# Weights issued later, block sums taken earlier, and half of one batch's q turned by DMA instead of TensorE

## The chip, the cores and the metric

One core of a Trainium2 chip. The metric is device time in microseconds (us) of one execution. Every run is listed with its granted TensorE clock (1.0 is full speed). Runs are sorted into fast and slow (slow: over 1.5% above the fastest run of the same kernel).

## The reference, cut to what matters

```python
# q, k, v: (4 batches, 8 heads, 768 positions, 64), float32
k_sum = k.reshape(B, H, 24, 32, D).max(axis=3)      # one key per block of 32
v_sum = v.reshape(B, H, 24, 32, D).mean(axis=3)     # one value per block
scores = [scale * q @ k.T  where |i - j| < 16,  scale * q @ k_sum.T + log(32)]
a = softmax(scores);  x = a @ [v, v_sum]            # (3072 tokens, 512)
h = x @ w_in                                        # w_in: 512 x 2048
out = (h * sigmoid(1.702 * h)) @ w_out              # w_out: 2048 x 512
```

Attention is sparse and small; the two dense products are what TensorE spends its time on (of the chain that ended last in the kernel before, `h` has 33.4% and `out` 36.4%).

## The kernel before

The tokens are taken in eight half-batches of 384, called stages 0 to 7. Each stage is a first layer (`ph`, 64 matmuls) and an output product (`po`, 48). Attention of the next half-batch is threaded between the steps of the output product. Each engine has its own instruction order, and in the traces it keeps to it (SP before, stages 1 and 2: k from 68.22 us, v from 75.17, k's transposes from 84.32, x's from 92.29, as the program has them). SP (SyncE) issues nearly all transfers, also the DMA transposes that turn q, k and x.

The opening, in GpSimd's order: two weight chunks go out between value casts.

```python
    load_w_in(0)                 # GpSimd issues the transfer
    s_mask(1, dve)
    v_even(1, "dve_alone")
    s_exp(2)
    load_w_in(1)
    v_before(2, pool)            # a cast on GpSimd that waits for value rows
# ... last value casts on GpSimd, each behind its transfer ...
    load_w_in(2); load_w_in(3); load_q(0, p, 1); load_w_out(0..3)
```

Batch 1's q is turned on TensorE in stage 1 (24 turns of 128 x 128, six per head pair: three for each half of the positions); batches 2 and 3 use SP transposes:

```python
    def tq1(p, eng):                       # batch 1, head pair p
        big = psb.tile([128, 1024], F32, name="ps_q", tag="big")
        for half in range(2):
            for r in range(JH):            # JH = 3
                pe.matmul(out=big[...], lhsT=src[:, r]..., rhs=ident)
        copy(eng, qT[p][1]..., big...)
    # plan1: which attention piece stands behind which step of stage 1's output product
    plan1 = {0: ["t0"], 1: ["t1"], 2: ["s0", "s1"], 4: ["t2"], 5: ["t3"], ..., 9: ["v1", "S0", "S1"], 11: ["x1"]}
```

And SP's order in an odd stage: k of the next batch behind step 1, its v behind step 7, then k's transposes, then the transposes of this attention's x (`xT`), which the next first layer reads.

The softmax here doesn't subtract the row's maximum and nothing guards it: scores larger than these inputs give would overflow.

Of the kernel before, what the change touches and what calls it, by code (L numbers as in the profile page):

```python
# [34 lines left out]
def kernel(  # L35
# [16 lines left out]
    NP = H // 2  # L52
# [45 lines left out]
    def load_q(b, p, half=None):  # L98
        if half is None:
            t = stage.tile([128, 2, NJ, D], F32, name=f"qf{p}", tag=f"qf{p}0")  # L100
            sp.dma_start(out=t.rearrange("p h j d -> p (h j) d"), in_=chunks(q, b, p))
            raw["q", p] = t
            return
        if half and p == 0:
            late[0] = stage.tile([128, NP, 2, JH, D], F32, name="qfl", tag="qfl")
            if b == 0:
                pool.dma_start(out=late[0].rearrange("p i h r d -> p (i h) (r d)"),
                               in_=q[0, :, HALF:S].rearrange("h (p r) d -> p h (r d)", r=JH))
        t = (late[0][:, p] if half else
             stage.tile([128, 2, JH, D], F32, name=f"qf{p}0", tag=f"qf{p}0"))  # L110
        raw["q", p, half] = t
        if b == 0 and half:
            return
        sp.dma_start(out=t.rearrange("p h r d -> p h (r d)"),
                     in_=q[b, 2 * p:2 * p + 2, half * HALF:(half + 1) * HALF]
                     .rearrange("h (p r) d -> p h (r d)", r=JH))
# [135 lines left out]
    def copy(eng, out, in_):  # L252
        if eng is act:
            act.activation(out=out, in_=in_, func=ACT.Copy)
        elif eng == "dve_alone":

            dve.tensor_reduce(out=out, in_=in_.unsqueeze(len(in_.shape)), axis=AX.X, op=ALU.max)
        else:
            eng.tensor_copy(out=out, in_=in_)
# [13 lines left out]
        cast["k", p] = t  # L273

    def cast_q1(p):
        for half in range(2):
            cast_q(pool, p, half)
            cast["q", p, half] = cast.pop(("q", p))

    def cast_q(eng, p, half=None):  # L280
        if half is None:
            if p % 2 == 0:
                qb2[p // 2] = castp2.tile([128, 2, NJ, 2, D], BF16, name="qb", tag="qb")
            t = qb2[p // 2][:, p % 2]
        else:
            t = castp.tile([128, JH, 2, D], BF16, name="qb", tag="qb")
        copy(eng, t.rearrange("p r h d -> p h r d"),
             raw[("q", p) if half is None else ("q", p, half)])
        cast["q", p] = t
# [207 lines left out]
    def b_exp(g):  # L497
        ab = st["ab", g] = attp.tile([128, HALF], BF16, name="ab", tag="ab")
        act.activation(out=ab, in_=st["B", g][:, 0:HALF], func=ACT.Exp, scale=scale)

    def v_own(p, hh, eng):

        copy(eng, rows_of(0, p, hh)[:, :, 1], raw_v(p, hh))
# [4 lines left out]
    def v_before(p, eng):  # L508

        copy(eng, rows_of(0, p)[96:128, 1:JH, 0], raw_v(p)[96:128, 0:JH - 1])  # L510
# [97 lines left out]
        key_rows(p, s, ks)  # L608

    def tq1(p, eng):  # L610
        big = psb.tile([128, 1024], F32, name="ps_q", tag="big")
        for half in range(2):
            src = cast.pop(("q", p, half))
            for r in range(JH):
                o = half * 512 + r * 128
                pe.matmul(out=big[:, o:o + 128], lhsT=src[:, r].rearrange("p h d -> p (h d)"),
                          rhs=ident, start=True, stop=True)
        copy(eng, qT[p][1].rearrange("p (e c r) -> p e r c", e=2, r=JH),
             big.rearrange("p (e x) -> p e x", e=2)[:, :, 0:HALF]
             .rearrange("p e (r c) -> p e r c", r=JH))  # L620

    a_sb, x_sb, x2 = {}, {}, {}

# [189 lines left out]
    v_own(1, 1, "dve_alone")  # L813
    av_near(0)
    av_blocks(0, 0, D + 1)
    load_w_in(0)
    s_mask(1, dve)
    v_even(1, "dve_alone")
    s_exp(2)
    load_w_in(1)  # L820
    v_before(2, pool)
    v_sum(1)
    v_copy(1, act)
    v_own(2, 1, "dve_alone")
# [55 lines left out]
    for p in range(NP):  # L880
# [2 lines left out]



    plan = {0: ["s0", "s1"], 3: ["v0", "s2", "s3"], 4: ["d0"], 5: ["v1", "S0", "S1", "d1"]}
    odd = {0: ["v0", "s2", "s3"], 1: ["d0"], 3: ["v1", "d1"]}

    plan1 = {0: ["t0"], 1: ["t1"], 2: ["s0", "s1"], 4: ["t2"], 5: ["t3"],
             6: ["v0", "s2", "s3"], 8: ["x0"], 9: ["v1", "S0", "S1"], 11: ["x1"]}  # L890

    plan0 = {-1: ["q0", "q1", "q2", "q3", "s0", "s1"], 3: ["v0", "s2"], 5: ["x0", "s3"], 7: ["v1"], 9: ["x1"]}

# [1 line left out]

    def beside(u, slot):
        b, half = u // 2, u % 2
        for what in (plan0 if u == 1 else plan1 if u == 2 else odd if half else plan).get(slot, ()):
            i = int(what[1])
            if what[0] == "t":  # L900
                tq1(i, dve if i % 2 else act)
            elif what[0] == "q":
                q_turn(i, 1)
                q_copy(i, dve, 1)
            elif what[0] == "s":
                scores(b, half, i)
                if half and i == NP - 1:
                    gelu_soon()
            elif what[0] == "S":
                scores(b, 1, i)  # L910
                if i == 1:
                    gelu_soon()
            elif what[0] == "v":
                values(b, half, i, u == 1)
            elif what[0] == "d":
                dx(i)
            else:
                tx(i)
# [25 lines left out]
    for u in range(2 * B):  # L944
        b, half = u // 2, u % 2
        todo = {}
        if u == 0:
            for p in range(NP):
                todo.setdefault(12 + p // 2, []).append(lambda p=p: cast_q(dve, p, 1))
        elif u == 1:  # L950
            s = 1
            todo = {2: [lambda: tk(0, s)], 4: [lambda: tk(1, s)],
                    6: [lambda: tk(2, s)], 8: [lambda: tk(3, s)],
                    14: [lambda: halo_odd(w51, 0), lambda: vsum(s, range(NJ))],
                    15: [lambda: block_sums(), lambda: halo_even(w51, 0),
                         lambda: sum_dmas(w51, 0)]}
            for p in range(NP):
                cast_k(pool, p)
            for p in range(NP):
                cast_v(pool, s, p, 0)  # L960
                cast_v(pool, s, p, 1)
            for p in range(NP):
                cast_q1(p)
        elif half == 0 and b + 1 < B:
            todo = {0: [lambda: turn_keys(u, b + 1)]}
        elif b + 1 < B:
            s = (b + 1) % 2
            todo = {0: [lambda: turn_queries(u, s)],
                    1: [lambda: rest_k(0, s)], 3: [lambda: rest_k(1, s)],
                    6: [lambda: rest_k(2, s)], 8: [lambda: rest_k(3, s)]}  # L970
        if u == 1:
            for p in range(NP):
                clear_kx(pool, p, 0)
            clear_vw(pool, 0)
        if u:
            ff_in(u, range(3))
        for nt in range(0 if u else N0, NT):
            if u == 0 or nt > 2:
                ff_in(u, (nt,))
            for f in todo.get(nt, ()):  # L980
                f()
        nxt = u + 1 < 2 * B
        if nxt:
            exp_soon()
        if u == 0:
            beside(1, -1)
            busy(6)
        i = 0
        order = [(ms, part) for ms in range(JH) for part in range(4)]
        if u == 0:  # L990

            order = [(ms, part) for part in range(4) for ms in range(JH)]
        for ms, part in order:
            if nxt or ms < JH - 1:
                ff_out(u, ms, part)
            elif part == 0:
                ff_last(u, ms)
            if nxt:
                beside(u + 1, i)
            i += 1  # L1000
            if u == 0 and i == 1:

                sp.dma_start(out=hold, in_=w_out_sb[0:16, NT - 5, 0:16])
                for p in range(NP):
                    load_k(1, p)
                load_v(1)
                for p in range(NP):
                    load_q(1, p, 0)
                    load_q(1, p, 1)
            elif half and b + 2 < B and i == 1:  # L1010
                for p in range(NP):
                    load_k(b + 2, p)
            elif half and b + 2 < B and i == 7:
                load_v(b + 2)
            elif half == 0 and 0 < b < B - 1 and i == 7:
                for p in range(2, NP):
                    load_q(b + 1, p)
            elif half == 0 and 0 < b < B - 1 and i == 10:
                s = (b + 1) % 2
                vsum(s, range(NJ))  # L1020
                block_sums()
                w5 = vw[s].rearrange("p (j e) h c -> p j e h c", e=2)
                halo_dmas(w5, 0)
                sum_dmas(w5, 0)
# [30 lines left out]
```

## Time and profile before

| | kernel before |
|---|---|
| median, range | 219.09 us, 217.85 to 220.0 (3 runs) |
| profiled span | 218.5 us, clock 0.998 |
| TensorE busy | 205.6 us, 94% |
| idle of TensorE one can name | 1.9 (value rows), 0.5 (w_in), 0.6 (q's copy) us |

The prediction below shows the lines. Lines of SP's queue give start, time held, queue, kind, tiles, count.

### The profile page before, as it was taken

How to read it: one execution, taken by the hardware profiler on the slowest of the kernel's cores; microseconds unless marked ns; L12 is line 12 of the kernel's file. 1: busy time of each engine (PE TensorE's matmuls, PEld its weight loads, DVE VectorE, ACT ScalarE, POOL GpSimd, SP SyncE). 2: the span in 40 equal slices, each digit the busy share in tenths (PEclk: the TensorE clock that was granted, in tenths of full speed). 3: DMA queues.
4: the chain of work that ended last, by engine and by line, in shares of the span. 5: the costliest groups of instructions: out<-in, count | busy, mean ns of one | idle time of the engine just before them, and what ended most of it. 6: DMA issues, size and time to landing. Idle time of an engine off the chain costs nothing.

```text
span 218.5 us, 4915 instructions
## 1 busy us (share of the span) xinstructions
PE 205.6 (94%) x1927; PEld 116.0 (53%) x1950; DVE 91.0 (42%) x262; ACT 135.5 (62%) x242; POOL 68.8 (32%) x169
## 2 busy tenths in 40 slices
PE   7785998999999999999999999999999999999994
PEld 3354655456655555545555465545655555456542
DVE  5897708443964840336707300619228003300000
ACT  2797868156578397842786677815787578437420
POOL 5684988014974019500600069004100000000000
PEclk9999999999999999999999999999999999999999
DMA  5999999999998999899799999989904300520012
GB/s 163 317 217 195 139 263 215 192 196 218 233 352 196 225 252 236 142 221 226 148 204 222 217 227 194 205 194 204 197 3 104 115 0 3 120 92 7 0 48 96
DMA packets 92710, 37.15 MB, mean 170 GB/s; under 512 B 77856, under 2 KB 89568, under 8 KB 92688
## 3 DMA queue, kind: packets, MB, share of 16 engines
q1 hardware_dynamic: 88272, 31.87, 71.0%
q0 software_dynamic: 4416, 4.98, 13.2%
q8 instruction: 15, 0.25, 0.5%
q14 instruction: 7, 0.06, 0.1%
HBM read 27.26 MB, written 6.29 MB: 154 GB/s over the span
## 4 chain that ended last, share of the span: by engine, by line
PE 79%; DMA 10%; SPq 6%; issue 2%; POOL 2%; DVE 1%; POOLq 0%; DVEq 0%
PE po L27 36%; PE ph L27 33%; DMA w_out_sb<-in_moe_w_out_dram 7%; SPq L27 6%; PE ps_av L27 3%; DMA vf<-in_v_dram 3%; PE ps_s L27 3%; PE ps_t L27 1%; DVE qT L27 1%; POOL w_in_sb L27 1%; PE ps_q L27 1%; PE ps_vs L27 1%; PE ps_x L27 1%; POOL vw L27 0%; POOL qfl L27 0%
## 5 line engine op out<-in xcount | busy, mean ns | idle before, releaser
L27 PE MATMUL po<-w_out_sb,gT 128*128 128x512 bf16 (+2 forms) x377 | 85.7, 370 | 2.4 <-issue 1.8
L27 PE MATMUL ph<-xT,w_in_sb 128*128 128x384 bf16 x512 | 85.8, 326 | 0.5 <-DMA w_in_sb<-in_moe_w_in_dram 0.5
L27 ACT ACTIVATE gT<-ph 128x384 bf16<-128x384 f32 x128 | 61.1, 491 | 23.1 <-PE ph L27 23.1
L27 PEld LDWEIGHTS <-w_in_sb 128*128 128x128 bf16 x512 | 49.6, 98 | 33.8 <-DMA w_in_sb<-in_moe_w_in_dram 1.1
L27 PEld LDWEIGHTS <-gT 128*128 128x128 bf16 x400 | 36.5, 98 | 39.1 <-issue 0.3
L27 ACT ACTIVATE osb<-po 128x512 f32<-128x512 f32 (+1 forms) x24 | 14.1, 589 | 35.0 <-PE po L27 33.6
L27 ACT ACTIVATE a_sb<-ps_s 128x768 bf16<-128x768 f32 x32 | 24.3, 804 | 12.7 <-PE ps_s L27 12.4
L27 DVE RECIPROCAL rc<-ps_av 128x6 f32<-128x6 f32 x32 | 6.1, 190 | 50.5 <-PE ps_av L27 50.4
L27 POOL CAST vw<-vf 128x768 bf16<-128x768 f32 (+4 forms) x35 | 24.7, 765 | 5.0 <-DMA vf<-in_v_dram 3.8
L27 DVE TENSOR_TENSOR a_sb<-a_sb,mk 128x768 bf16<-128x768 bf16 x32 | 17.9, 563 | 17.5 <-ACT a_sb L27 15.9
L27 ACT ACT_TABLE_LOAD x16 | 20.5, 1283 | 1.1 <-PEq L1039 0.8
L27 POOL COPY gate<-gT 128x1 bf16<-128x1 bf16 x4 | 0.8, 192 | 60.2 <-ACT gT L27 60.2
L27 DVE TENSOR_TENSOR x<-ps_av,rc 128x384 bf16<-128x384 f32 x28 | 15.6, 558 | 1.0
L27 POOL CAST kb<-kf 128x768 bf16<-128x768 f32 (+1 forms) x15 | 11.1, 768 | 15.5 <-DMA kf<-in_k_dram 15.5
L27 PEld LDWEIGHTS <-a_sb 128*64 128x64 bf16 x384 | 8.0, 111 | 6.4 <-issue 3.1
L27 DVE COPY osb<-po 128x128 f32<-128x128 f32 x1 | 0.3, 292 | 26.6 <-PE po L27 26.6
L27 DVE TENSOR_REDUCE ks<-kx 128x24 bf16<-128x768 bf16 x12 | 11.2, 938 | 0.1
L27 PE MATMUL ps_s<-qT,kx 64*128 64x64 bf16 x384 | 9.3, 191 | 1.0 <-DVE qT L27 0.6
L27 PE MATMUL ps_av<-vw,a_sb 128*64 128x65 bf16 x384 | 10.0, 197 | 0.1
L27 POOL CAST qb<-qf 128x768 bf16<-128x768 f32 (+1 forms) x14 | 9.4, 698 | 1.5 <-DMA qf<-in_q_dram 0.9
L27 DVE COPY kx<-kx 128x80 bf16<-128x80 bf16 (+4 forms) x50 | 9.6, 287 | 0.0
L27 PEld LDWEIGHTS <-kx 64*128 64x128 bf16 x384 | 7.0, 95 | 3.8 <-issue 3.0
(71 smaller groups left out, 121.6 us busy)
## 6 DMA issues: line engine op xcount, KB each, us to landing
out_dram<-osb SPq DMA_DIRECT2D x23, 256.0 KB, 3.3
kf<-in_k_dram SPq DMA_DIRECT2D x12, 384.0 KB, 5.5
vf<-in_v_dram SPq DMA_DIRECT2D x12, 384.0 KB, 6.3
qf<-in_q_dram SPq DMA_DIRECT2D x8, 384.0 KB, 4.9
w_in_sb<-in_moe_w_in_dram POOLq DMA_DIRECT2D x4, 512.0 KB, 8.2
w_out_sb<-in_moe_w_out_dram POOLq DMA_DIRECT2D x4, 512.0 KB, 16.2
kf<-in_k_dram SPq DMA_DIRECT2D x8, 192.0 KB, 3.9
qf<-in_q_dram SPq DMA_DIRECT2D x8, 192.0 KB, 5.3
```

The lines of the kernel that those rows point to most:

```text
L27: r = f(*a, **kw)
```

## The change

Its intent: keep the weights out of the way of the last value rows (the "hold-back" below), take twelve transposes and half of each of four PSUM copies out of TensorE's full stage (the late half of batch 1's q, "late q" below, goes by DMA), and move one block of scores and the block sums to places where nobody waits for them. Its core (the copies of the plans and the cast are cut):

```diff
+    def pool_waits(p):
+        pool.tensor_copy(out=gate2, in_=a_sb[p][:, 0, 0, 0:1])   # a gate: one column
...
+    s_mask(1, dve)
+    pool_waits(1)
     load_w_in(0)
-    s_mask(1, dve)
     v_even(1, "dve_alone")
     s_exp(2)
+    v_before(2, pool)
     load_w_in(1)
-    v_before(2, pool)
...
+    def xq1(p):                                   # late half of batch 1's q, pair p
+        sp.dma_start(out=qT[p][1][:, HALF:S]..., in_=late_q(p)..., transpose=True)
...
     def tq1(p, eng):                              # now 3 matmuls, not 6
...
-    plan1 = {0: ["t0"], 1: ["t1"], 2: ["s0", "s1"], 4: ["t2"], 5: ["t3"],
-             6: ["v0", "s2", "s3"], 8: ["x0"], 9: ["v1", "S0", "S1"], 11: ["x1"]}
+    plan1 = {0: ["t0", "t1"], 2: ["s0", "s1"], 4: ["t2", "t3"],
+             6: ["v0", "s2", "s3"], 8: ["x0"], 9: ["v1"], 11: ["x1"]}
+    plan3 = {2: ["s0", "s1"], 4: ["v0", "s2", "s3"], 5: ["d0"], 6: ["v1", "d1"]}
...
-            busy(6)                               # six filler matmuls in the opening
...
             elif half and b + 2 < B and i == 1:
+                if u == 1:                        # stage 1
+                    for p in range(NP):
+                        load_q(1, p, 1)           # three transfers on SP
                 for p in range(NP):
                     load_k(b + 2, p)
+                if u == 1:
+                    for p in range(NP):
+                        cast_q1(p)
+                        xq1(p)                    # four transposes on SP, three tiles each
...
+            elif half == 0 and 0 < b < B - 1 and i == (6 if u == 2 else 4):
+                vsum((b + 1) % 2, range(NJ))      # was at step 10, with the sums
```

More of the change, by code (lines that the diff above doesn't have):

```diff
@@ L112, in load_q @@
         if b == 0 and half:
+            return
+        if half:
+            if p == 0:
+                for r in range(JH):
+                    o = HALF + r * 128
+                    sp.dma_start(out=late[0][:, :, :, r].rearrange("p i h d -> p (i h) d"),
+                                 in_=q[b, :, o:o + 128].rearrange("h p d -> p h d"))
             return
@@ L275, in cast_q1, with late_q @@
     def cast_q1(p):
-        for half in range(2):
-            cast_q(pool, p, half)
-            cast["q", p, half] = cast.pop(("q", p))
+        if p == 0:
+            qb2[0] = castp2.tile([128, 2, NJ, 2, D], BF16, name="qb", tag="qb")
+        pool.tensor_copy(out=late_q(p).rearrange("p r h d -> p h r d"), in_=raw["q", p, 1])
+    def late_q(p):
+        return qb2[0][:, p // 2, p % 2 * JH:p % 2 * JH + JH]
+    def xq1(p):
+        sp.dma_start(out=qT[p][1][:, HALF:S].rearrange("p (j c) -> p j c", c=128),
+                     in_=late_q(p).rearrange("p r h d -> p (r h d)"), transpose=True)
     def cast_q(eng, p, half=None):
@@ L610, in tq1 @@
     def tq1(p, eng):
-        big = psb.tile([128, 1024], F32, name="ps_q", tag="big")
-        for half in range(2):
-            src = cast.pop(("q", p, half))
-            for r in range(JH):
-                o = half * 512 + r * 128
-                pe.matmul(out=big[:, o:o + 128], lhsT=src[:, r].rearrange("p h d -> p (h d)"),
-                          rhs=ident, start=True, stop=True)
-        copy(eng, qT[p][1].rearrange("p (e c r) -> p e r c", e=2, r=JH),
-             big.rearrange("p (e x) -> p e x", e=2)[:, :, 0:HALF]
-             .rearrange("p e (r c) -> p e r c", r=JH))
+        ps = pmm.tile([128, 512], F32, name="ps_q", tag="mm")
+        src = cast.pop(("q", p))
+        for r in range(JH):
+            pe.matmul(out=ps[:, r * 128:r * 128 + 128],
+                      lhsT=src[:, r].rearrange("p h d -> p (h d)"), rhs=ident, start=True, stop=True)
+        copy(eng, qT[p][1][:, 0:HALF].rearrange("p (c r) -> p r c", r=JH),
+             ps[:, 0:HALF].rearrange("p (r c) -> p r c", r=JH))
     a_sb, x_sb, x2 = {}, {}, {}
@@ L882 @@
     clear_vw(pool, 1)
-    plan = {0: ["s0", "s1"], 3: ["v0", "s2", "s3"], 4: ["d0"], 5: ["v1", "S0", "S1", "d1"]}
+    plan = {1: ["s0", "s1"], 3: ["v0", "s2", "s3"], 4: ["d0"], 5: ["v1", "S0", "S1", "d1"]}
+    plan3 = {2: ["s0", "s1"], 4: ["v0", "s2", "s3"], 5: ["d0"], 6: ["v1", "d1"]}
     odd = {0: ["v0", "s2", "s3"], 1: ["d0"], 3: ["v1", "d1"]}
-    plan1 = {0: ["t0"], 1: ["t1"], 2: ["s0", "s1"], 4: ["t2"], 5: ["t3"],
-             6: ["v0", "s2", "s3"], 8: ["x0"], 9: ["v1", "S0", "S1"], 11: ["x1"]}
+    plan1 = {0: ["t0", "t1"], 2: ["s0", "s1"], 4: ["t2", "t3"],
+             6: ["v0", "s2", "s3"], 8: ["x0"], 9: ["v1"], 11: ["x1"]}
     plan0 = {-1: ["q0", "q1", "q2", "q3", "s0", "s1"], 3: ["v0", "s2"], 5: ["x0", "s3"], 7: ["v1"], 9: ["x1"]}
@@ L897, in beside @@
         b, half = u // 2, u % 2
-        for what in (plan0 if u == 1 else plan1 if u == 2 else odd if half else plan).get(slot, ()):
+        for what in (plan0 if u == 1 else plan1 if u == 2 else plan3 if u == 3 else odd if half else plan).get(slot, ()):
             i = int(what[1])
@@ L906, in beside @@
                 scores(b, half, i)
-                if half and i == NP - 1:
+                if i == NP - 1 and (half or b == 1):
                     gelu_soon()
@@ L962 @@
             for p in range(NP):
-                cast_q1(p)
+                cast_q(pool, p, 0)
         elif half == 0 and b + 1 < B:
@@ L1008 @@
                     load_q(1, p, 0)
-                    load_q(1, p, 1)
             elif half and b + 2 < B and i == 1:
+                if u == 1:
+                    for p in range(NP):
+                        load_q(1, p, 1)
                 for p in range(NP):
                     load_k(b + 2, p)
+                if u == 1:
+                    for p in range(NP):
+                        cast_q1(p)
+                        xq1(p)
             elif half and b + 2 < B and i == 7:
@@ L1017 @@
                     load_q(b + 1, p)
+            elif half == 0 and 0 < b < B - 1 and i == (6 if u == 2 else 4):
+                vsum((b + 1) % 2, range(NJ))
+            elif half == 0 and 0 < b < B - 1 and i == (8 if u == 2 else 5):
+                block_sums()
             elif half == 0 and 0 < b < B - 1 and i == 10:
                 s = (b + 1) % 2
-                vsum(s, range(NJ))
-                block_sums()
                 w5 = vw[s].rearrange("p (j e) h c -> p j e h c", e=2)
```

## The prediction

> **What bounds the kernel now.** I read the busy shares first, then the chain that ended last in order of time, then every idle stretch of TensorE, then the DMA issues with their landings.
>
> ```profile
> span 218.5 us, 4915 instructions
> PE 205.6 (94%) x1927; PEld 116.0 (53%) x1950; DVE 91.0 (42%) x262; ACT 135.5 (62%) x242; POOL 68.8 (32%) x169
> PE 79%; DMA 10%; SPq 6%; issue 2%; POOL 2%; DVE 1%; POOLq 0%; DVEq 0%
> ```
>
> TensorE (PE) is busy 94% of the span and is 79% of the chain; only about 13 us of idle are left. The chain says where a gain can be had. Its early part:
>
> ```profile
> 14.12 6.10 DMA vf<-in_v_dram
> ...
> 20.27 0.52 POOL vw L27
> ...
> 20.84 0.34 PE ps_vt L27 x3
> ...
> 21.30 0.50 POOL vw L27
> 21.80 1.44 POOL w_in_sb L27 x2
> 23.23 0.90 POOL qfl L27
> ...
> 24.85 15.31 DMA w_out_sb<-in_moe_w_out_dram
> 40.16 0.04 issue
> 40.20 1.02 PE po L27 x4
> ```
>
> The last value rows (vf) land at 20.22, GpSimd (POOL) casts them, and only behind that cast does it issue the last two chunks of w_in, the late q and all of w_out. Chunk 2 of w_out lands at 40.16 and TensorE goes on there. The 15.31 us is not one transfer's length: the chunk stands in a queue behind four others. From 40.2 on the chain is TensorE nearly all the way, except here:
>
> ```profile
> 64.44 0.86 PE po L27 x4
> 65.30 0.35 PE ps_q L27 x6
> 65.65 0.02 issue
> 65.67 1.46 DVE qT L27
> 67.13 0.04 issue
> 67.17 0.35 PE ps_s L27 x12
> ```
>
> This is the output product of the second half-batch (stage 1; stages count half-batches from 0), with batch 1's attention interleaved. Scores wait for VectorE to copy the transposed q out of PSUM. TensorE's own list of idle times agrees:
>
> ```profile
> PE ps_vt L27 <- POOL vw L27: 2.2, 2, 1.9
> PE ph L27 <- DMA w_in_sb<-in_moe_w_in_dram: 0.5, 1, 0.5
> PE ps_s L27 <- DVE qT L27: 0.6, 2, 0.4
> ```
>
> The first is the wait for the last value rows, up to 20.84; the second the wait for w_in's third chunk at 29.09; the third is two waits at 36, behind the last q turns of batch 0. The stall at 66 shows in the idle list only as two shorter gaps (0.19 and 0.13 us) because matmul ends are modelled; the chain gives its size. The gaps of 0.16 us before an output product that the page names "issue" I take for lost records: there the group has 7 or 23 matmuls where the program has 8 or 24. DMA is busy to the full until 43 and heavily loaded to 102:
>
> ```profile
> 22.00:24.00 2.00, 1.78 (x28) 1.27 (x24) 1.71 (x5) 1.64 (x3) 2.00 (x3) 1.00 0.66 65
> 24.00:34.00 10.00, 9.49 (x60) 5.49 (x58) 2.70 (x18) 7.39 (x17) 9.03 (x27) 1.00 1.15 228
> ```
>
> The columns before the last two are engine times and clock, the last are DMA share and GB/s. Between 22 and 24 DMA falls to 65 GB/s, because w_in's second pair was issued only at 21.75. That hole is what the held-back load can close.
>
> [...]the first w_in packets appear at 16.7; of the 16 engines' reports on the last vf transfer twelve come by 17.66, the last three at 18.91, 19.03 and 20.22. [...]The kernel before already does it: its twelve-tile qT transposes hold the SP queue about 2.1 us and its six-tile xT ones 1.2 us. [...]
>
> **The change part by part.**
> 1. *w_in held back.* A one-column GpSimd copy of the second masked score tile comes ahead of w_in's first load. That tile is ready at 16.14 in the trace, so the load goes at about 16.4 and not 14.51; the second goes behind one more value cast, at about 17.7 and not 15.38. The value rows then have DMA to themselves: most engines finish at 17.2 to 17.7 already, and the slowest, which was 0.5 us behind the rest for the earlier value loads, should at 18.1 and not 20.22. The wait of 1.86 us does not vanish, as GpSimd becomes its end: 17.7 + 0.75 (issue) + 1.15 (two casts) + 0.5 = 20.05. So block sums 0.8 us earlier, and w_in's second pair issued at 21.0.
>  Against this w_in starts 1.9 us later. In the third w_in chunk most engines report 5.0 to 5.4 us after the issue and the slowest after 7.3, with no value rows beside it. So the first chunk lands between 22.5 and 23.7 (before: 21.92). I take 23.1: TensorE wants it at about 21.7, and here a new wait of some 1.4 us takes the old one's place. From there the queue runs with no hole at the 2.54 us per chunk that the slowest engine shows (29.05 to 31.60): w_in at 25.6, 28.2, 30.7; late q 2.15 later, 32.9; first w_out 3.6 later (value-row copies share this stretch), 36.5; second 2.83 later, 39.3 in place of 40.16. TensorE: 62 first-layer matmuls of 163 ns after about 23.9 end at 34.0, then q turns and scores take 1.95 (2.6 before, less 0.65 waiting), 36.0. It then meets w_out at 36.5, and after twelve matmuls (2.58) at 39.1 its second chunk at 39.3. **Gain: 0.85 us**, set by w_out.
> 2. *Six filler matmuls gone* (0.47 us on the path before w_out). They only shorten TensorE's way to the same landing: worth nothing beyond point 1.
> 3. *Half of batch 1's q no longer turned on TensorE.* 24 transposes become 12. Six take 0.34 us, so 4 x 0.17 = **0.68 us** off a stage with TensorE fully busy. ACT's and VectorE's copies halve from 1.46 us to about 0.7. With both first transposes one step earlier, scores at step 2 no longer wait: the output product ends at 66.50, scores could end at 66.96 and end at 67.52: **0.56 us**.
> 4. *Late q's route.* Three loads of 256 KB go behind the value-row copies, then four GpSimd casts (0.51 each), then four SP transposes (three tiles, about 0.7 each). Half the q traffic leaves the stretch around 55 to 62, where SP was late (its value-row copies went out only at 63.5), so SP gets there about 2.5 us sooner and spends that again on late q and the transposes. K of batch 2 is about level, its V about 2 us later than now. The use of late q is some 25 us on: hidden.
> 5. *Scores of the second half of batch 1* move from stage 1 to step 2 of stage 2: 0.46 us moved, not saved.
> 6. *Block sums* for batches 2 and 3 come earlier in stages 2 and 4: the same 0.45 us of TensorE, and VectorE's 4.4 us of waiting for them (DVE 100.30) is idle time off the path.
> 7. *Scores one step later in stages 3 and 5:* exp waits for its table until 114.4 in any case, so nothing.
>  Cost: with attention of stage 2 starting at step 2, its last transposed x is issued about 3.4 us before the next first layer wants it, against 4.4 now; landing takes 4.1 (median). First use of that half is about 1 us into the stage. I charge **+0.2 us** for it.
>
> Sum: -0.85 -0.68 -0.56 +0.2 = -1.9 us; 219.09 - 1.9 = **217.2 us**.
>
> **The rivals.**
> - *The held-back weights cost as much as they give.* If w_in's first chunk needs 7.4 us from its issue, it lands at 23.8 and w_out's second at 40.0. The first part is then worth 0.1 to 0.3, total about 217.8. For it: both w_in pairs show one engine some 2 us behind the others. Against: the first pair's laggard still had value rows to drain.
> - *Everything follows the value rows.* If w_in's slowest engine was late only through the value rows, the first chunk lands at about 21.8 and w_out's second at about 38.4: 1.8 us, total about 216.2.
> - *SP becomes the bound.* SP issues in order, and each transpose waits for a GpSimd cast, which waits for three loads. If late q comes slowly, the output store, V of batch 2, K's transposes and at the end x's transposes of stage 2 all slip; TensorE would stand 2 to 4 us at stage 3's first layer: 219 to 221. For it: SP issues nearly without a break from 63.5 to 84. Against: SP still waits for x there (the issue at 92.29 takes 3.28 us, a later unhindered one 1.22).
>
> **Range and chances.** First part 0.1 to 1.8, second 1.0 to 1.3, third -0.0 to +2 (mostly near 0.2); three runs of before spread over 217.85 to 220.0, another 0.3 us or so of the median. So 215.6 to 219.0 eight times in ten. Faster by 2% means under 214.7, which needs 4.4 us, while all the idle that the change can reach (2.2 + 0.5 + 0.6 + 0.56) and the work removed (0.68 + 0.47) make 5.0, most of it ahead of w_out's landing: 5%. Slower by 2% needs the third rival much worse than I drew it: 2%.
>
> **What would show it.** Step 1: the last vf landing near 18, value casts of the last pair ending near 20.0, a wait for w_in's first chunk in place of the 1.9 us, w_out's second chunk at 39 to 39.6. Steps 2 and 3: no matmuls on ps_w behind the opening, 12 on ps_q in stage 1, no wait of scores for qT at 66, stage 1's output product 1.2 us shorter besides the 0.46 that moves. Step 4: transposes of late q landed by 80. Cost: idle at the start of stage 3's first layer, on xT. I am wrong if w_in's first chunk lands outside 22.5 to 23.7, if a new wait of over 0.5 us appears from 63 on, or if SP is late with xT.

## More of the kernel before

The `xT` rows are what stage 3's first layer waits for.

```profile
68.22 5.12 SPq L27 DMA_DIRECT2D kf<-in_k_dram  x4
73.44 1.68 SPq L27 DMA_DIRECT2D out_dram<-osb  x1
75.17 7.20 SPq L27 DMA_DIRECT2D vf<-in_v_dram  x4
...
84.32 6.06 SPq L27 DMA_TRANSPOSE kx<-kb  x4
...
92.29 3.28 SPq L27 DMA_TRANSPOSE xT<-x  x1
...
96.29 1.27 SPq L27 DMA_TRANSPOSE xT<-x  x1
```

Then TensorE at that place: the first layer follows the output product without a gap and takes 10.56 us to its last end.

```profile
100.18 1.90 PE L27 MATMUL po<-w_out_sb,gT 128*128 128x512 bf16 x8
101.92 10.56 PE L27 MATMUL ph<-xT,w_in_sb 128*128 128x384 bf16 x64
```

## The result, and the profile after

226.29 us median of 4 runs (225.37 to 228.36), against 219.47 for the kernel before in the same rounds. The ratio is 1.034, 95% interval 1.024 to 1.043. Ratios here and below are the mean time of one kernel's fast runs over the mean of the other's fast runs of the same rounds, so they are not quite the ratio of the medians. The profiled span is 225.0 us at clock 0.983.

The page of the kernel after, engine shares and the granted clock by slice (40 slices of 5.6 us): TensorE is busy for 4.3 us more although it has less to do, and one slice is at half clock. Of the 4.3 us some is only record-keeping: the trace before holds 377 of the 400 matmuls of the output product and shows 1.8 us of idle time there that no wait explains, the trace after holds all 400.

```profile
PE 209.9 (93%) x1932; PEld 115.9 (52%) x1932; DVE 87.9 (39%) x262; ACT 134.4 (60%) x242; POOL 70.8 (31%) x170
...
PEclk9999999999999999998599999999999999999999
```

The list of TensorE's waits (us in total, times, longest) of the kernel after: what was 1.9 us for value rows is now 0.9, and a wait that the kernel before did not have stands at the top.

```profile
PE ph L27 <- DMA xT<-x: 4.7, 1, 4.7
...
PE ps_vt L27 <- POOL vw L27: 1.2, 2, 0.9
```

SP's queue of the kernel after, the same part as before:

```profile
65.85 2.38 SPq L27 DMA_DIRECT2D qfl<-in_q_dram  x3
68.27 7.29 SPq L27 DMA_DIRECT2D kf<-in_k_dram  x4
75.66 7.58 SPq L27 DMA_TRANSPOSE qT<-qb  x4
...
84.20 4.85 SPq L27 DMA_DIRECT2D vf<-in_v_dram  x4
...
91.41 6.39 SPq L27 DMA_TRANSPOSE kx<-kb  x4
...
101.29 2.60 SPq L27 DMA_TRANSPOSE xT<-x  x2
```

K of batch 2 goes out at the same time in both kernels (68.2 and 68.3). V goes out 9.0 us later (84.20 against 75.17), of which the four new transposes hold SP for 7.58. V's own issue is then shorter, K's transposes still start 7.1 us later (91.41 against 84.32), and x is handed to DMA at 101.29 and 102.67. VectorE had written the last of x at 97.99 (95.87 before), so it is SP that is late more than x. Nor did SP stand waiting for the casts of late q, as the prediction's third rival allowed for: they ended at 74.25, before the first of the four transposes went out.

```profile
72.06 2.19 POOL L27 CAST qb<-qfl 128x384 bf16<-128x384 f32 x4 [6.55 <-DMA qfl<-in_q_dram]
```

While SP was busy with the last of the four transposes DMA had nearly nothing to do: between 80 and 82 us (same view as the first stretches in the prediction; the last two columns are DMA share and GB/s) it moved 6 GB/s, where the kernel before moved 219.

```profile
80.00:82.00 2.00, 2.00 (x14) 1.22 (x13) 0.00 (x0) 1.52 (x4) 1.72 (x3) 1.00 0.05 6
...
106.00:112.00 6.00, 6.00 (x21) 2.90 (x20) 0.00 (x0) 1.97 (x4) 2.85 (x5) 0.54 1.26 223
```

The second of these lines has the granted clock (third column from the right): 0.54 in the six us behind the wait. TensorE at that place:

```profile
96.56 4.49 PE L27 MATMUL po<-w_out_sb,gT 128*128 128x512 bf16 x20
105.77 13.39 PE L27 MATMUL ph<-xT,w_in_sb 128*128 128x384 bf16 x64 [4.72 <-DMA xT<-x]
119.00 1.89 PE L27 MATMUL po<-w_out_sb,gT 128*128 128x512 bf16 x8
```

The sum is short. At the end of stage 2 the kernel after is 0.9 us ahead (101.05 against 101.92). It waits 4.72 us. The 64 matmuls then take 13.23 us from start to the next group's start in place of 10.40 (101.92 to 112.32), because the clock is halved for 6.83 us, from 104.73 on (the first 1.04 us of it still fall into the wait): 2.83 us more. So -0.87 + 4.72 + 2.83 = 6.7 us behind at 119.00 against 112.32, and from there on both keep step to the end (225.0 against 218.5).

The half-clock stretch here is 6.83 us long; those in the openings are 3.41 us (f2, g2) or twice that (h2). At this place it came with idles of TensorE of 4.7, 4.9 and 6.0 us (the change, g1, e1), and with none of 1.1 to 2.2 us. In e1, a run below, the clock fell 2.5 us after TensorE had gone idle (99.53 to 102.05). The length of a wait does not tell by itself: in the opening the clock fell in some runs with no longer wait than 1.3 us (f2), and not in the kernel before, which waits 1.86 us. Nor does the busy time of the 3.41 us ahead of the fall: TensorE was busy for 0.90 us of them in e1, 1.26 in g2 and 1.88 in f2, and a stretch as long with 1.70 us busy (h5, 102.18 to 105.59) kept the full clock. So these traces give no clean limit.

The stage in front went as predicted. Stage 1 from its first output matmul to stage 2's first layer took 15.7 us before (63.1 to 78.8) and takes 13.9 now (62.5 to 76.4): 1.8 us, of which 0.46 has moved to stage 2.

### The profile page after: what moved, and what is told of

Its sections match the earlier page's. It is cut to its first block, busy times and chain, and to the rows that moved or that the text cites.

```text
span 225.0 us, 4910 instructions
## 1 busy us (share of the span) xinstructions
PE 209.9 (93%) x1932; PEld 115.9 (52%) x1932; DVE 87.9 (39%) x262; ACT 134.4 (60%) x242; POOL 70.8 (31%) x170
## 4 chain that ended last, share of the span: by engine, by line
PE 64%; DMA 20%; POOL 6%; SPq 3%; issue 3%; DVE 2%; ACT 0%; POOLq 0%; DVEq 0%
PE ph L27 29%; PE po L27 28%; DMA w_out_sb<-in_moe_w_out_dram 7%; DMA vf<-in_v_dram 5%; SPq L27 3%; PE ps_av L27 3%; DMA kx<-kb 2%; PE ps_s L27 2%; POOL vw L27 2%; DMA qfl<-in_q_dram 2%; DMA xT<-x 2%; DMA kf<-in_k_dram 2%; POOL kb L27 1%; POOL qb L27 1%; PE ps_vt L27 1%
## 5 line engine op out<-in xcount | busy, mean ns | idle before, releaser
L27 PE MATMUL ph<-xT,w_in_sb 128*128 128x384 bf16 x512 | 88.6, 333 | 4.7 <-DMA xT<-x 4.7
L27 PE MATMUL po<-w_out_sb,gT 128*128 128x512 bf16 (+2 forms) x400 | 88.5, 371 | 0.7 <-DMA w_out_sb<-in_moe_w_out_dram 0.7
L27 PEld LDWEIGHTS <-w_in_sb 128*128 128x128 bf16 x512 | 50.4, 100 | 40.2 <-issue 8.2
L27 DVE TENSOR_TENSOR a_sb<-a_sb,mk 128x768 bf16<-128x768 bf16 x32 | 19.7, 621 | 49.0 <-ACT a_sb L27 47.4
L27 POOL CAST vw<-vf 128x768 bf16<-128x768 f32 (+4 forms) x35 | 26.3, 795 | 9.1 <-DMA vf<-in_v_dram 8.4
L27 PE MATMUL ps_av<-vw,a_sb 128*64 128x65 bf16 x384 | 10.4, 198 | 1.0 <-POOL vw L27 0.6
L27 DVE COPY kx<-kx 128x80 bf16<-128x80 bf16 (+4 forms) x50 | 8.2, 258 | 0.0
```

The lines of the kernel that those rows point to most:

```text
L27: r = f(*a, **kw)
```

## The experiments

My theory: the four small transposes hold SP's queue and everything behind them (theory 1 in the expectations below), and the half clock behind the wait adds to it. Rivals: late q's transfers take DMA bandwidth from K and V (theory 2); x itself is late, as stage 2's attention starts at step 2 (theory 3). Eighteen runs of sixteen kernels were made (h3 repeats f1, h5 repeats h4); all of them gave correct results.

| run | kernel | median us | ratio to before | 95% interval |
|---|---|---|---|---|
| - | the change | 226.29 | 1.0337 | 1.0243 to 1.0430 |
| e1 | transposes behind V | 227.44 | 1.0361 | 1.0297 to 1.0426 |
| e2 | late q turned on TensorE | 221.94 | 1.0095 | 1.0050 to 1.0139 |
| e3 | one transpose for four | 222.67 | 1.0167 | 1.0103 to 1.0232 |
| e4 | change + filler at stage 3 | 228.21 | 1.0382 | 1.0307 to 1.0457 |
| f1 | before + hold-back | 222.14 | 1.0146 | 1.0092 to 1.0199 |
| h3 | the same again | 221.52 | 1.0061 | 1.0020 to 1.0101 |
| f2 | before - opening's filler | 219.09 | 0.9993 | 0.9960 to 1.0026 |
| f3 | late q on TensorE, no hold-back | 219.54 | 1.0017 | 0.9990 to 1.0044 |
| f4 | before + q turned in pairs | 219.50 | 0.9985 | 0.9955 to 1.0014 |
| g1 | change, no hold-back | 224.80 | 1.0245 | 1.0189 to 1.0301 |
| g2 | before, second chunk held | 219.22 | 0.9986 | 0.9956 to 1.0015 |
| h1 | before, first chunk held | 220.09 | 1.0026 | 0.9995 to 1.0057 |
| h2 | before, gate copy alone | 219.99 | 1.0006 | 0.9970 to 1.0043 |
| g3 | before, third chunk early | 218.88 | 0.9992 | 0.9970 to 1.0014 |
| g4 | the same, q in pairs | 218.80 | 0.9990 | 0.9961 to 1.0019 |
| h4 | change, no hold-back, filler | 225.68 | 1.0254 | 1.0196 to 1.0313 |
| h6 | one transpose, no hold-back | 220.70 | 1.0007 | 0.9973 to 1.0040 |

(The kernel before: 219.46, 219.68, 219.42, 219.41 and 219.75 us median in the rounds concerned. The ratios hang on which runs count as slow, most where a kernel has few: the runs listed as fast give 1.0124 for f1, 1.0077 for h3 and 1.0198 for h4, whose slow runs are three of six. h5 was not timed over rounds.)

### Where the transposes stand in SP's order

```diff
                 if u == 1:
                     for p in range(NP):
                         cast_q1(p)
-                        xq1(p)
             elif half and b + 2 < B and i == 7:
                 load_v(b + 2)
+                if u == 1:
+                    for p in range(NP):
+                        xq1(p)
```

> The changed kernel with one edit: the four small transposes of batch 1's late q stand on the SP queue behind batch 2's V loads and no longer ahead of stage 1's output store and those loads. Theory 1 (SP issues in order; the four transposes hold it for 7.6 us at 75.7 to 83.2 while the DMA engines run dry, and all behind them slips to stage 2's transposes of x): V of batch 2 is issued from about 76 and not 84.2, the DMA hole at 79 to 84 closes, x's last transpose is issued at 98 to 100 and not 102.7, the wait for xT at stage 3 shrinks from 4.7 to 0 to 2 us and the halved clock (6.8 us long, 3.0 us lost) goes with it: 219 to 221 us. Theory 2 (late q's three loads put 768 KB ahead of K and V and DMA bandwidth is what is short): bytes and their order hardly change, wait stays 4 us or more, 225 to 227 us. Theory 3 (attention of stage 2 starts at step 2, so x itself is late): no change, 226 us.

Measured 227.44 us, 1.036. V now goes out at 77.16, seven us earlier than in the change, the four transposes then hold SP for 6.72 us at 83.41, and x is handed over at 100.83; TensorE waits 6.0 us and the clock is halved behind it. By its time this is a miss of theory 1 (219 to 221) and what theories 2 and 3 said; but V's early start and the 6.72 us on SP say that V was not what was late. What counts is SP's time ahead of x's transposes, wherever it is spent; the next run sets that apart from theories 2 and 3.

### Late q without the transposes

The transfers and casts of the change stay; the late half is turned by twelve matmuls and four VectorE copies in steps 0 and 1 of stage 2.

```diff
-                        xq1(p)
+    def tq1b(p, eng):      # three matmuls against ident, then copy to qT[p][1][:, HALF:S]
-    plan3 = {2: ["s0", "s1"], ...
+    plan3 = {0: ["T0", "T1"], 1: ["T2", "T3"], 2: ["s0", "s1"], ...
```

> The changed kernel without the four transposes of late q on the SP queue: late q is loaded and cast as in the change, but turned by 12 TensorE matmuls and four VectorE copies at steps 0 and 1 of stage 2. Theory 1: no wait for xT at stage 3 (0 to 0.5 us), clock full throughout, TensorE pays 0.68 us for the turns: 218 to 219.5 us, or 217.5 if nothing else waits. Theory 2: late q's loads are still ahead of K and V, so a wait of 3 to 5 us stays: 224 to 227 us. Theory 3: the attention plan is the same, so the wait stays at 4 to 5 us: 226 us.

Measured 221.94 us, 1.010. The wait for x is 1.06 us, no half clock, x is handed over at 96.89. The four instructions on SP are therefore worth 2.4% (1.0337 less 1.0095), and the transfers and casts are not the cause. But a loss of nearly 1% was left (theory 1 had said 218 to 219.5 us), which none of my theories had.

### One instruction for four

```diff
-        sp.dma_start(out=qT[p][1][:, HALF:S]..., in_=late_q(p)..., transpose=True)     # x4, 3 tiles
+        if p == NP - 1:
+            sp.dma_start(out=q1v[:, 1]..., in_=qb2[0]..., transpose=True)              # x1, 12 tiles
```

(batch 1's q is kept half by half so that one instruction can write all of it.)

> The changed kernel with the four three-tile transposes of late q made one twelve-tile transpose of the same bytes at the same place of the SP queue (the q buffer of batch 1 is laid out half by half). Theory 1 in its form 'each transpose costs SP about 1.2 us whatever its size, plus waits': one takes 2.1 to 3 us in place of 7.6, V of batch 2 is issued from about 79, the wait for xT falls from 4.7 to about 0 to 1 us, clock full: 218 to 220 us. If the cost goes by tiles or bytes: 7 us again and 225 to 227 us. Theories 2 and 3: 225 to 227 us.

SP's queue of this run, the same twelve tiles in one instruction:

```profile
76.47 3.54 SPq L27 DMA_TRANSPOSE qT<-qb  x1
...
80.69 5.86 SPq L27 DMA_DIRECT2D vf<-in_v_dram  x4
...
98.83 2.84 SPq L27 DMA_TRANSPOSE xT<-x  x2
```

3.54 us for 7.58; V goes out 3.5 us and x 2.5 us earlier than in the change, TensorE waits 1.35 us, no half clock. The time: 222.67 us, 1.017. It misses the 218 to 220 expected; the hold-back, still in this run, turned out to be part of that. The cost of a transpose on SP was mostly one of the instruction here. Shortest single durations in all traces: three tiles 1.18 us (the first two of the four took 2.21 and 2.66), six tiles 1.21, twelve tiles 1.66.

### The half clock

Seventy filler matmuls ahead of stage 3's first layer, so that TensorE does not sit idle while it waits:

```diff
+        if u == 3:
+            busy(70)
         if u:
             ff_in(u, range(3))
```

> The changed kernel with 70 filler matmuls of 128 columns (about 3.9 us) ahead of stage 3's first layer, where TensorE stands idle for 4.7 us. If the idle time itself makes the granted clock fall to half afterwards, the clock stays full, stage 3's first layer takes 10.4 us and not 13.4: 223 to 224 us, 3 us less than the change. If the clock falls for another reason, 226 us or a little more.

The first layer is back at 10.4 us (108.1 to 118.5), the gap in front is 0.21. The time is 228.21 us all the same (223 to 224 expected). In the profiled run the layer also started 2.4 us later than in the change, behind two half-clock stretches of 3.4 us, at 21.6 and 38.7; that these account for the time is not shown.

### The parts alone

Four kernels, each one edit on the kernel before, but for the third, which is the run with late q on TensorE less the hold-back (and with the opening's filler back):

```diff
f1:  the diff of the opening above, nothing else
f2:  -            busy(6)
f3:  load order and busy(6) of the kernel before put back into "late q on TensorE"
f4:  -    plan1 = {0: ["t0"], 1: ["t1"], 2: ["s0", "s1"], 4: ["t2"], 5: ["t3"],
     +    plan1 = {0: ["t0", "t1"], 2: ["s0", "s1"], 4: ["t2", "t3"],
```

> The kernel before with the held-back w_in load alone. The kernel without the small transposes on SP (e2) is still 0.95% (2.1 us) above before, though its profile shows every stage from 1 to 7 together only 0.5 us longer than before's; so some 1.5 us should be lost in the opening. Theory A: the hold-back loses it (w_in and all of w_out behind it later in most runs, and more runs with a 3.4 us window of halved clock in the opening): 1.0 to 2.0 us above before, ratio 1.005 to 1.009, clock below 1.0 in most runs. Theory B (as in the prediction): the hold-back gains: 0.3 to 0.9 us below before, ratio 0.996 to 0.999. Theory C: neither, within 0.3 us.

> The kernel before without the six filler matmuls ahead of stage 0's output product. Prediction's step 2: worth nothing, ratio 0.998 to 1.002. Theory F (the filler kept TensorE busy enough in the opening to keep the clock full): 0.5 to 1.7 us above before, with clock windows in more runs than before's, ratio 1.003 to 1.008.

> The kernel of e2 (late q turned on TensorE, no small transposes on SP) with w_in loaded as early as in before and the six filler matmuls back, so that its opening is before's. If the opening parts lose the 1.5 us: ratio 1.000 to 1.004 (219.3 to 220.3 us), stage 1 about 2.2 us shorter, given back in stage 2 by 0.46 moved, 0.68 of turns and 1 us of wait for xT. If they do not, ratio 1.008 to 1.011 as e2 and the loss must lie in stages 1 to 3.

> The kernel before with one line changed: batch 1's q is turned two pairs at a time at steps 0 and 4 of stage 1 and no longer one pair at steps 0, 1, 4 and 5; all loads, all 24 transposes and the early scores of the second half stay. Prediction's step 3, its second term alone (scores at step 2 no longer wait for VectorE's copy of q): 0.3 to 0.6 us below before, ratio 0.997 to 0.9985. If the wait only moves (both PSUM slots of the transposes are busy when the scores want them): ratio 0.999 to 1.002.

The filler is worth nothing (0.9993), as predicted. q in pairs takes the wait at 66 us away in the trace and leaves 0.15% (interval from 0.45% less to 0.14% more), unclear. Late q on TensorE without the hold-back is level with the kernel before (1.0017). The hold-back alone costs: 1.0146, more than the 1.005 to 1.009 of the theory that had it lose. So the missing 1% is the part that I had predicted to gain. Yet the profile of that run, its fastest (219.66 us), showed no loss anywhere.

### The hold-back taken apart

```diff
g2, second chunk:  load_w_in(1) behind v_before(2), load_w_in(0) where it was, no gate
h1, first chunk:   gate, load_w_in(0), load_w_in(1), then v_before(2)
h2, gate alone:    both loads where they were, then the gate copy, then v_before(2)
h3:                the whole hold-back again, for more runs and a second profile
```

> The kernel before with half of the hold-back: only the second w_in chunk goes behind one more value cast, the first stays where it was, no gate. Theory that holding back moves the hole in DMA use rather than closing it (the value rows alone keep DMA at about 120 to 140 GB/s in 16 to 20 us where 180 to 200 flowed with w_in beside them): a small loss or none, since w_in's first chunk fills the stretch: ratio 1.000 to 1.006. Rival, that what costs is the extra GpSimd work (gate copy and order of casts): ratio below 1.002 and no change of the landings. If half the delay costs as much as the whole (1.010 and over), both fall.

> The kernel before with the other half of the hold-back: the gate on the second masked score tile and w_in's first chunk behind it, the second chunk directly after. Holding back the second chunk alone gave 0.9986, the whole 1.0146. If it is the late start of the first chunk that costs (DMA half empty from 16 to 20 us while the slowest engine still drains value rows): ratio 1.008 to 1.015, w_in's first chunk landing 0.5 to 1 us later than in the kernel before. If the two halves only cost together: 1.000 to 1.005.

> The kernel before with the gate's GpSimd copy alone, put behind both w_in loads, so that both loads go out as before and only GpSimd's next value cast waits for the masked score tile. If the loads' delay is what costs: ratio 0.998 to 1.003. If it is the coupling of GpSimd to the attention's mask: 1.008 to 1.015, as for the whole hold-back.

> The whole hold-back on the kernel before once more, to have more runs than six and a second profile, as the first profile was of its fastest run and showed no loss. If the loss is real: ratio 1.008 to 1.018, and the profile shows stage 0 to start or end over 1 us later than in the kernel before, or half-clock windows in the opening. If the six runs were a bad draw: 1.000 to 1.006.

Second chunk alone 0.9986, gate alone 1.0006, first chunk alone 1.0026, the whole again 1.0061 (221.52 us median of 11; with the first six runs, 17 runs around 221.7). The loss is real, as the interval of the whole (1.0020 to 1.0101) excludes none, smaller than the first six runs said and than the 1.008 to 1.018 expected, and mostly there only when both chunks are late: for each half alone the interval includes no loss. The rival "the two halves only cost together" is the better reading, though it is not shown, as the intervals of h1 and h3 overlap; the gate's copy is cleared.

The second profile is one of a more usual run (span 219.8 at full clock). Stretches of the opening (columns as above, the last two are DMA share and GB/s), 16 to 18 us of the kernel before:

```profile
16.00:18.00 2.00, 1.69 (x35) 1.50 (x33) 1.86 (x5) 1.85 (x6) 0.65 (x3) 1.00 1.10 179
```

The same stretch, and that of 22 to 24 us, of the second hold-back run:

```profile
16.00:18.00 2.00, 1.47 (x23) 1.33 (x23) 2.00 (x5) 1.94 (x5) 1.62 (x4) 1.00 0.55 89
...
22.00:24.00 2.00, 1.90 (x15) 1.22 (x16) 1.67 (x8) 1.93 (x4) 2.00 (x3) 1.00 1.30 197
```

The hole at 22 to 24 us (65 GB/s in the kernel before, a line of the prediction) is gone, and a new one stands at 16 to 18: the value rows, with DMA to themselves, do not fill it (89 GB/s, 179 in the kernel before). And TensorE waits for the weight chunks as they come (start, time, tiles, count, and the idle in front with its releaser):

```profile
25.73 2.77 PE L27 MATMUL ph<-xT,w_in_sb 128*128 128x384 bf16 x16 [0.41 <-DMA w_in_sb<-in_moe_w_in_dram]
28.91 2.77 PE L27 MATMUL ph<-xT,w_in_sb 128*128 128x384 bf16 x16 [0.40 <-DMA w_in_sb<-in_moe_w_in_dram]
...
35.47 0.34 PE L27 MATMUL ps_q<-ident,qb 128*128 128x128 bf16 x3 [0.82 <-DVE qb L27]
```

Late q of batch 0 lands at 34.80 (33.75 before), and stage 0's output product starts at 38.99 in place of 37.38.

The profiles taken together say the same. Eight of them have the kernel before's loading order (the kernel before, f2, f3, f4, g1, h4, h5, h6) and eight hold the first chunk back (the change, e1 to e4, f1, h1, h3). DMA moves on average, in GB/s:

| us | 16-18 | 18-20 | 20-22 | 22-24 | w_out's second chunk lands at |
|---|---|---|---|---|---|
| as before (8) | 198 | 201 | 206 | 121 | 38.87 (37.39 to 40.16) |
| held back (8) | 115 | 135 | 193 | 190 | 39.95 (39.17 to 40.91) |

Times two us each, holding back loses (83 + 66 + 13) x 2 = 324 KB in the first three stretches and wins 69 x 2 = 138 KB in the last: 186 KB, by estimate 0.9 us at the 200 GB/s or so of the first row, and the landing is 1.1 us later. Note the kernel before's own profile: 65 GB/s in the hole and 40.16 for the landing are the second worst and the worst of the eight. (h1's profile is of a slow run; without it the held-back mean is 39.89.) These are averages over different kernels, so they show where the loss can come from, not its size.

### The change without the hold-back

```diff
     the opening and busy(6) of the kernel before, all else as in the change
```

> The whole change with the four small transposes, but the kernel before's loading order of w_in and its six filler matmuls back: the missing corner of the two-by-two of hold-back and transposes. Adding up the earlier runs (change 1.034, change with the late q turned on TensorE 1.010, the same without the hold-back 1.002) the small transposes are worth +2.4% and the hold-back +0.8%. Theory that the two add up: ratio 1.020 to 1.028, about 224.5 us, TensorE idle of 4 to 5 us at the first layer of stage 3 and a granted clock near half for two windows of 3.4 us there. Rival, that the idle comes from both together (a later opening pushes the DMA queue of SP late): ratio under 1.012 and less than 2 us of idle there.

1.0245, TensorE idle for 4.87 us at stage 3, clock halved for 6.8 us behind it, the first layer 12.96 us long (105.10 to 118.06). The two parts add up: 2.4% for the transposes, 0.9% for the hold-back. (Between e2 and f3 the hold-back is worth 0.8%, between e3 and h6 1.6%, alone 0.6 to 1.5%.)

### One transpose without the hold-back

```diff
     both edits above: one transpose of twelve tiles, opening of the kernel before
```

> The change without the hold-back and with one transpose of twelve tiles in place of four of three (q of batch 1 kept half by half so that one instruction can write it). With the hold-back one transpose gave 1.0167 and four 1.0337; four without it gave 1.0245. If the hold-back is worth the same about 1% everywhere: ratio 1.004 to 1.010, no half clock at stage 3 and an idle of under 2 us there. If the one transpose costs as much as the four once the hold-back is gone: 1.018 and over. If it costs nothing: under 1.003.

1.0007. Less than the expected 0.4 to 1.0%, although TensorE still waits in stage 3, 1.35 us for x and 1.26 us for the q of batch 2, whose transposes also stand behind in SP's order (handed over at 110.21, 106.83 in the kernel before):

```profile
101.92 10.56 PE L27 MATMUL ph<-xT,w_in_sb 128*128 128x384 bf16 x64 [1.35 <-DMA xT<-x]
...
115.46 0.53 PE L27 MATMUL ps_s<-qT,kx 64*128 64x64 bf16 x24 [1.26 <-DMA qT<-qb]
```

So with one instruction in place of four the route by DMA is level with the kernel before: what it takes off stage 1 it pays back in these two waits (the profiled run, 221.81 us, is one of the slower ones). The median over all of its 22 runs, fast and slow, is 220.70, 0.4% over the kernel before's 219.75, so I call it level and no better.

### Filler again, without the hold-back

The filler of above on the change without the hold-back; then the same kernel for a second look.

> The change without the hold-back (ratio 1.0245, TensorE idle 4.9 us ahead of stage 3, then two half-clock windows), with 70 filler matmuls put ahead of stage 3's first layer, so that TensorE is not idle while it waits for the transposed x. The filler takes some 4.6 us and covers the wait. If the half clock behind the idle is worth the 3.0 us that the longer layer shows: 1.3 to 1.6% less, ratio 1.008 to 1.013, stage 3's first layer back to 10.4 us. If the clock is lost wherever the wait is: 1.020 and over.

> A second look at the filler run without the hold-back, which was 222 to 229 us from run to run, most of them at a full clock, and profiled in its fastest run. If what varies is the TensorE idle in front of stage 3 (SP's queue reaching x's transposes at different times): a time of over 224 us goes with a first layer of stage 3 that starts over 2 us later than the 103.1 of the first look, at an unchanged 10.4 us for the layer. If it varies elsewhere: stage 3's first layer starts within 1 us of the first look and the time is lost in another stage.

1.0254: no gain on 1.0245, against the 1.3 to 1.6% expected, a miss. Three of the six runs are listed as slow; the three fast ones average 223.6 us, the six of the change without the hold-back 224.6, so half a per cent of gain is not excluded. In both looks the first layer of stage 3 is 10.4 us long at full clock. The second:

```profile
99.81 4.07 PE L27 MATMUL ps_w<-warm 128*128 128x128 bf16 x70
106.06 10.56 PE L27 MATMUL ph<-xT,w_in_sb 128*128 128x384 bf16 x64 [2.18 <-DMA xT<-x]
```

The first look (221.94 us, the fastest of its six runs) started this layer at 103.12, the second (224.72 us) at 106.06: the time went with the start, which waited for x in both (SP handed x over at 97.76 and 99.88). So these two runs differ by when x arrives, and by as much as the half clock is worth. That the clock is halved with the idle and not with filler in its place, and that the layer takes 1.6 (e1) to 2.8 us longer for it, is shown in the traces; that taking it away would shorten the kernel by as much is not shown.

### The hole filled from the other side

If the hole in front of w_in's third chunk is what costs, it can be closed by issuing that chunk earlier instead of the others later: GpSimd has 1.25 us of waiting in front of its last own-row value cast.

```diff
+    load_w_in(2)
     v_own(3, 1, pool)
...
-    load_w_in(2)
     load_w_in(3)
-            busy(6)
```

and the same with q turned in pairs.

> The reverse of the hold-back on the kernel before: w_in's third chunk is issued by GpSimd ahead of its last own-row value cast, where GpSimd stands 1.25 us waiting for the last value rows, so that it queues behind the second chunk and the DMA hole at 22 to 24 us (65 GB/s) closes; the filler is left out. If the hole is what w_out's landing pays for, w_out's second chunk lands about 1 us earlier (38.5 to 39.2), the 0.5 us wait for w_in's third chunk is gone, and the time falls by 0.4 to 1.0 us: ratio 0.9955 to 0.998. If the value rows are slowed by it or TensorE is what binds from 20.8 on: ratio 0.999 to 1.003.

> The run before it and the two first turns of batch 1's q side by side in stage 1 (which alone gave 0.9985, unclear). Adding up: 0.6 to 1.4 us below the kernel before, ratio 0.9935 to 0.997, and no wait of scores for the copied q at 66. If both only shift waits: 0.998 to 1.001.

In the two profiles DMA moves 176 and 198 GB/s in 22 to 24 us, and w_out's second chunk lands at 37.93 and 37.90, 0.9 us ahead of the mean of the eight. The times are 0.9992 and 0.9990: nothing that can be told from the kernel before. With the weights early, TensorE no longer waits for them in these traces; it still waits 1.4 us for the last value rows at 20.3, and the rest of the opening is its own work. No version here beats the kernel before by more than the scatter.

## Why the prediction was wrong

Predicted 217.2 us (215.6 to 219.0), 2% for slower; it came out at 226.29.

- **Step 4, late q's route, is the step that failed.** It read "four SP transposes (three tiles, about 0.7 each)" and "hidden". 2.8 us were charged, 7.58 were measured, and the shortest of the four took 1.18. The 0.7 was an estimate, the straight line through six tiles at 1.2 us and twelve at 2.1, carried down to three; three tiles take what six take (1.18 and 1.21 us at the least). The kernel before showed it: its own four K transposes of six tiles held SP for 6.06 us, 1.37 to 1.50 each (the line at 84.32), and its xT ones took 1.21 to 3.28, so "1.2" was the least of its kind and 2.1 for twelve tiles about the middle (1.95 to 2.74). And the argument looked at when late q is needed, 25 us on, not at what stands behind it in SP's order: V, k's transposes, x's transposes. The change without hold-back (1.0245) against one transpose without it (1.0007) settles that it is the number of instructions: the same bytes, casts and place in the order, one instruction for four. V came 9.0 us later and not "about 2 us later".
- **The third rival had the mechanism**, "x's transposes of stage 2 all slip; TensorE would stand 2 to 4 us at stage 3's first layer: 219 to 221". The wait was 4.72 us. It was given little weight ("mostly near 0.2"). What it did not have is the clock, which was halved with that wait, so that the layer took 2.83 us more. Its counter-argument, that SP still waits for x there in the kernel before, was worth 3.28 - 1.27 = 2.0 us, against 9.0 us that SP fell behind.
- **Step 1, the hold-back.** The landings were right within half a us: w_in 25.6, 28.2, 30.7 predicted, 25.65, 28.20, 30.97 in the profile of the change; late q 32.9 and 33.18; w_out's second chunk 39.3 and 39.80. Only the first w_in chunk came earlier than I feared (22.07 for 23.1, outside the 22.5 to 23.7 that the prediction had named as a sign of being wrong). That the next ones agree is partly luck: they were reckoned from 23.1 at 2.54 us a chunk, and the first step measured 3.58. (A small slip: 17.7 + 0.75 + 1.15 + 0.5 is 20.1, not 20.05.) The gain was wrong in sign: it was taken as 40.16 - 39.3, and 40.16 is the latest of eight profiles with that loading order. Against their mean of 38.87 the same 39.3 is a loss of 0.4 us, and the held kernels' mean of 39.95 one of 1.1. "That hole is what the held-back load can close" was the failing thought: the load moved the hole to an earlier stretch, as value rows alone moved 115 GB/s on average at 16 to 18 us, where value rows and weights moved 198.
- **The first rival of the prediction** (the weights cost as much as they give) was nearer, and went not far enough: about 0.6 to 1.5% is lost.
- **Step 2**, filler worth nothing: right (0.9993). **Step 3**: right in the trace. 0.68 + 0.56 + the 0.46 that moved is 1.7 us; stage 1 became 1.8 us shorter. How much of its 0.56 us (0.26%) reaches the end of an average run is not shown: q in pairs alone gave 0.9985, with 0.26% and nothing both inside the interval.
- **Step 6**, block sums: they wait in stage 2 for 0.26 us for V's casts now (V is late), beside 0.29 us for masked scores. Their worth by themselves was not tried, nor that of steps 5 and 7; the run with late q on TensorE and no hold-back contains them and is level.
- **The cost of 0.2 us** for x's late start: without transposes of late q on SP the wait for x was 1.06 us in e2 and none in f3.
- **The chance.** 2% for slower rested on the third rival being hardly worse than it was drawn, a stand of 2 to 4 us. The stand alone was 4.72 us; the 2.83 us of half clock behind it were in no rival.

Still open: how much of the 2.4% is the half clock, what makes x's arrival vary by 2.9 us between two runs of one kernel, and why the hold-back's halves cost less alone than together.

## What to carry to other kernels

Charge a new instruction in a full in-order queue to whatever stands last behind it (here x, 4.72 us of wait), and take its cost from instructions of its kind in a row in the trace (here four K transposes, 6.06 us), not from bytes or tiles: merging four small transposes into one took back nearly the whole 2.4% (1.0245 to 1.0007). Before a gain is read from one landing time, look at how far that landing differs between runs; a single profile can show the worst of eight. Before transfers are held back, see whether those that go first can fill DMA alone; here they did not (115 GB/s on average at 16 to 18 us, 198 with the weights beside them).
